# First batch of a Mamba-2 scan with mixer: B and x loaded with two neighbouring tokens to a partition, words reordered

## The chip, the cores and the metric

The kernel runs on one core of one Trainium2 chip. The metric is device time in microseconds (us). Five engines work beside each other, each through its own queue in order: TensorE (PE, with its weight loads PEld), VectorE (DVE), ScalarE (ACT), GpSimd (POOL) and SyncE (SP), whose queue issues nearly all of the DMAs. Engines wait for one another by semaphores.

## What is computed

Two stages follow each other. The first is a scan over 4 batches, 8 heads, 768 tokens, head size 32, state size 16; the second is a mixer over tokens and channels.

```
for each chunk:                       # cum = cumsum(log a) in the chunk
    M = (C B^T) * exp(cum_i - cum_j) * causal
    y = M x  +  (C state) * exp(cum)
    state = exp(sum log a) * state + sum_j exp(cum_last - cum_j) B_j x_j
u = y + (V^T U^T y)                   # along the tokens, rank 32; y as (768, 256)
out = u + relu(u w_ch1) w_ch2
```

The kernel picks its own chunks (64 tokens); the result is the same.

## The kernel before

The scan is cut into twelve *pairs* k = 0 to 11: three pairs of 256 tokens for each of four batches, each with four chunks of 64 tokens. Pairs 0, 1 and 2, the first batch, are called LIGHT and have code of their own; pairs 1, 2 and 3 are SCALED, their products of B and C with the decays are made on POOL (L490), all others on DVE. The steps of a pair:

- loads: `load_bc` (L199) takes B in two DMAs of 64 KB, one for each block of 128 tokens (runs of 64 bytes), and C in one of 128 KB, with tokens 2p and 2p+1 on partition p (runs of 128 bytes). `load_x` (L214) takes x in two DMAs of 128 KB, again a block each (runs of 128 bytes).
- `prep` (words P, Q): BC = B and C times decays F. The decays come from `decays` (L383, words A0 for B and A1 for C, over all four batches) and the chunk factors `kept` from `keep` (word K).
- `turn` (words T, V): transposes on PE, then copies T (ACT) and masked copies Cm (ACT or DVE).
- `gram` (word g): the products of C and B, four PSUM banks of 128x512, one for each pair of heads. For a light pair 16 matmuls with 256 columns.
- `mask` (words M, m): the causal mask. Of the four banks of a light pair DVE takes three with a bitwise and against `lower`, and the fourth goes by an ACT copy (L563) and then POOL: one affine_select over 128x512 (L564) and one memset of a quarter (L567).
- `state` (word s), `update` (word u): the chunk's own state on PE (L598), then on DVE one instruction for each chunk (S), then on POOL the masked states Sm (L626; DVE for later pairs).
- `inter` (words i, j): what the earlier state adds (L672); `intra` (word n): M times x, for light pairs 16 matmuls over all 128 partitions (L694), for the others 32 over 64 partitions (L704). `yout` (word y) copies to yT, `ytokens` (words t, O) transposes back to tokens.

For pairs that aren't light, the two chunks that share a partition row range write different banks, and the second half of `inter` may start only when all earlier products of the pair are done: `apart` (L631) puts a memset of the tile `settled` into POOL's queue, which waits for those products and for which PE waits.

The mixer of a batch (words p, q, a, then U, f, e, h, J, d) uses nearly all of PE's time from then on. Its weights are 64-bit floats which DVE and ACT turn into 32-bit ones piece by piece (word c, steps of `to_fp32`, L424; the pieces of a conversion are taken one by one; loads W, w, Z for V, z for U).

The order of all work is written out by hand, as words: LOADS (L35) is issued first, PLAN (L40) is then followed word by word, and each word puts its instructions at the end of the queues of the engines it uses. So an instruction's place in each queue is the place of its word. F words are matmuls on constants that keep PE busy. All PSUM tiles come from one pool of eight banks. DMAs use eight semaphores in turn, so that an issue on SP waits for the DMA eight before it to have landed.

## Time and profile before

| | us |
|---|---|
| median of three runs (lowest, highest) | 217.02 (216.36, 218.56) |
| the profiled execution: its time, its span | 216.94, 215.1 |
| busy in that span: PE, DVE, ACT, POOL | 207.0, 161.3, 119.9, 14.5 |

A time in a row of the timeline is the start in us from the span's start, then the time that it took; `x3` says that three instructions were merged, and brackets tell the idle time before it and what ended it. A matmul in 32 bits stands as two records. All of DVE's instructions bear the line of a helper, L169, so its rows are told apart by tile.

### The profile page before, as it was taken

What the parts mean: (1) busy time and instruction counts of PE and PEld (TensorE: products, weight loads), DVE (VectorE), ACT (ScalarE), POOL (GpSimd) and SP (SyncE); (2) the same over time, 40 slices, a digit from 0 to 9 for tenths busy, and PEclk for the clock granted to TensorE, in tenths of its full rate; (3) what the DMA queues carried; (4) which work ended last, traced back from release to release, by engine and by line L of the source; (5) the groups of instructions that cost most, each with busy time, mean ns of one, the idle gap of its engine ahead of it and who ended that gap; (6) DMA issues with size and microseconds to landing.
All of it is one profiled execution on the core that took longest, in us unless ns stands there. A gap on an engine that the chain in (4) does not pass through costs nothing.

```text
span 215.1 us, 6853 instructions
## 1 busy us (share of the span) xinstructions
PE 207.0 (96%) x2912; PEld 180.8 (84%) x2912; DVE 161.3 (75%) x334; ACT 119.9 (56%) x273; POOL 14.5 (7%) x46
## 2 busy tenths in 40 slices
PE   7998699999999999999999999999999999999993
PEld 4666465666676989999899999998999999999993
DVE  4679499999999999968977594497347756636942
ACT  3566567896847695655275527433646357357120
POOL 7463210000000000000000000000000000000000
PEclk9999999999999999999999999999999999999999
DMA  5987899998850035002061010100001000100012
GB/s 87 142 184 106 120 202 316 155 265 110 109 80 3 2 66 111 0 3 76 3 81 21 24 49 3 49 27 6 6 0 49 0 27 0 49 29 0 0 50 100
DMA packets 69519, 14.57 MB, mean 68 GB/s; under 512 B 63792, under 2 KB 67696, under 8 KB 69488
## 3 DMA queue, kind: packets, MB, share of 16 engines
q1 hardware_dynamic: 69488, 14.13, 33.6%
q8 instruction: 23, 0.38, 0.8%
q14 instruction: 8, 0.07, 0.1%
HBM read 10.98 MB, written 3.15 MB: 66 GB/s over the span
## 4 chain that ended last, share of the span: by engine, by line
PE 84%; SPq 5%; DMA 4%; DVE 2%; issue 2%; ACT 1%; DVEq 0%
PE x L797 31%; PE z L797 24%; PE y L797 12%; SPq L195 5%; PE y L704 3%; PE y L672 3%; DMA words<-in_moe_w_ch_dram 3%; PE x L547 2%; PE w L728 2%; PE w L506 2%; DMA bc<-in_C_dram 2%; PE w L598 1%; PE w L751 1%; PE z L547 1%; DVE M L169 1%
## 5 line engine op out<-in xcount | busy, mean ns | idle before, releaser
L169 DVE SCALAR_TENSOR_TENSOR words<-words 128x768 fp32r<-128x768 f32 (+6 forms) x48 | 38.0, 818 | 0.7 <-PE y L797 0.5
L797 PE MATMUL z<-u,w 128*128 128x384 f32 x144 | 32.0, 341 | 0.0
L797 PE MATMUL x<-u,w 128*128 128x384 f32 x144 | 31.7, 338 | 0.0
L797 PEld LDWEIGHTS z<-u,w 128*128 128x128 f32 x144 | 24.3, 188 | 0.3 <-issue 0.2
L797 PEld LDWEIGHTS x<-u,w 128*128 128x128 f32 x144 | 24.3, 188 | 0.2
L802 ACT ACTIVATE x<-x 128x384 f32<-128x384 f32 (+1 forms) x32 | 14.3, 448 | 18.1 <-PE x L797 18.1
L802 ACT ACTIVATE z<-z 128x384 f32<-128x384 f32 (+1 forms) x28 | 12.8, 461 | 16.6 <-PE z L797 16.1
L169 DVE SCALAR_TENSOR_TENSOR words<-x,words 128x384 fp32r<-128x384 f32 x24 | 13.1, 553 | 8.7 <-ACT words L831 8.6
L169 DVE SCALAR_TENSOR_TENSOR words<-z,words 128x384 fp32r<-128x384 f32 x24 | 12.9, 552 | 8.9 <-ACT words L831 8.8
L797 PE MATMUL y<-w,words 128*128 128x256 f32 x144 | 19.3, 281 | 0.0
L797 PEld LDWEIGHTS y<-w,words 128*128 128x128 f32 x144 | 18.4, 189 | 0.1
L797 PE MATMUL x<-w,words 128*128 128x256 f32 x128 | 18.3, 281 | 0.0
L797 PE MATMUL x<-w2c,words 128*128 128x256 f32 x96 | 17.6, 317 | 0.0
L797 PEld LDWEIGHTS x<-w,words 128*128 128x128 f32 x128 | 17.0, 188 | 0.2
L797 PEld LDWEIGHTS x<-w2c,words 128*128 128x128 f32 x96 | 14.9, 189 | 1.1
L831 ACT ACTIVATE words<-x 128x384 fp32r<-128x384 f32 x24 | 11.7, 491 | 6.0 <-PE x L797 5.9
L831 ACT ACTIVATE words<-z 128x384 fp32r<-128x384 f32 x24 | 11.6, 492 | 3.0 <-PE z L797 3.0
L169 DVE SCALAR_TENSOR_TENSOR S<-S,kept,w 128x64 f32<-128x64 f32 x40 | 11.1, 278 | 1.6
L797 PE MATMUL z<-yT,w1f 128*128 128x384 f32 x32 | 11.7, 495 | 0.1
L797 PE MATMUL x<-yT,w1f 128*128 128x384 f32 x32 | 11.1, 489 | 0.0
L672 PEld LDWEIGHTS y<-T,Sm 32*64 32x64 f32 x352 | 8.1, 131 | 2.7 <-issue 2.1
L797 PE MATMUL y<-w2c,words 128*128 128x256 f32 x72 | 10.3, 282 | 0.0
(170 smaller groups left out, 398.4 us busy)
## 6 DMA issues: line engine op xcount, KB each, us to landing
words<-in_moe_w_ch_dram SPq DMA_DIRECT2D x7, 512.0 KB, 6.8
x<-in_x_dram SPq DMA_DIRECT2D x24, 128.0 KB, 3.6
out_dram<-ytok SPq DMA_DIRECT2D x24, 128.0 KB, 1.7
bc<-in_B_dram SPq DMA_DIRECT2D x24, 64.0 KB, 3.0
bc<-in_C_dram SPq DMA_DIRECT2D x12, 128.0 KB, 3.1
words<-in_moe_w_ch_dram SPq DMA_DIRECT2D x2, 256.0 KB, 5.5
words<-in_moe_V_dram SPq DMA_DIRECT2D x4, 48.0 KB, 4.8
words<-in_moe_U_dram SPq DMA_DIRECT2D x1, 192.0 KB, 5.0
```

The source lines that it names most:

```text
L169: self.last = call(*args, **kwargs)
L195: op = nc.sync.dma_start(**kwargs)
L506: nc.tensor.transpose(out=tp[:, i, v], in_=s["BC"][:, i, c + v].rearrange("p h n -> p (h n)"), identity=ident)
L547: nc.tensor.matmul(out=g[r][cols, c], lhsT=s["T"][rows, 0, c, cols], rhs=s["Cm"][rows, :, :, ts(2 * c + p, Q)].rearrange("r v t i -> r v i ...
L598: nc.tensor.matmul(out=s["A"][p][ts(r, Q), v], lhsT=s["BC"][half, 0, v, 2 * r:2 * r + 2].rearrange("p h n -> p (h n)"), rhs=x_sb[k][half, ...
L672: product = nc.tensor.matmul(out=y[at][ts(r % 2, H), c, ts(p, H)] if light else y[p][ts(r % 2, H), r // 2, c], lhsT=own[ts(r, Q)], rhs=s[" ...
L704: product = nc.tensor.matmul(out=y[p][ts(i, Q), n, c], lhsT=x_sb[k][half, c, h], rhs=s["M"][half, h // 2, c, h % 2], start=fresh(k, p, [i] ...
L728: nc.tensor.transpose(out=t[:, c, g], in_=yT[b][:, g, ts(2 * q + c, P)], identity=ident)
L751: nc.tensor.matmul(out=p[ts(i % 4, Q), h], lhsT=U_sb[:, c], rhs=ytok[b][:, c, h], start=i < 4, stop=True, skip_group_check=True)
L797: nc.tensor.matmul(out=t, lhsT=lhsT, rhs=rhs, start=start, stop=True, skip_group_check=True)
L802: nc.scalar.activation(t, t, AF.Copy, scale=1.0 + EPS)
L831: nc.scalar.activation(gs[j, m // 2][0][:, m % 2], t, AF.Relu, scale=NEAR)
```

## The change

For the light pairs B and x now lie as C does: partition p holds tokens 2p and 2p+1. B comes in one DMA of 128 KB (runs of 128 bytes), x in one of 256 KB (runs of 256 bytes). LOADS now lists all nine DMAs of the first batch. What follows from the layout:

- `decays`: word A1 makes the factors for C and, by one more ACT instruction, the factors for B of batch 0. A0 is left with batches 1 to 3 and comes later.
- `prep`: for a light pair B in one instruction in place of two.
- masks: `lower` was filled by a memset and two copies on POOL. Now `paired` is made by two affine_selects over 64x256 and two memsets over 32x128 on POOL, and one DVE instruction over 128x256 turns it into `lower`. The fourth bank of a light pair takes two affine_selects over 64x512 and two memsets over 32x256 on POOL in place of one and one.
- `state`: a chunk is 32 partitions with two tokens each: 32 matmuls (32 rows, 32 columns, 64 wide) for a pair in place of 16, in two words s k.0 and s k.1, each with two PSUM banks of its own (four for a pair in place of two).
- `intra`: 32 matmuls over 64 partitions in place of 16 over 128; `inter` follows the new banks, and `apart` now holds for light pairs too: three more memsets on POOL and three more waits of PE.
- all words of PLAN up to about the first U words stand in another order; behind them few words change places.

```diff
 LOADS = (
-    'b0.0 b0.1 b0.2 x0.0 x0.1 b1.0 b1.1 b1.2 ')
+    'b0.0 b0.1 x0.0 b1.0 b1.1 x1.0 b2.0 b2.1 x2.0 ')
 PLAN = (
-    'x1.1 F2.0 A0 b2.1 Q1.0 Q0.0 A1 Q0.1 b2.2 Q1.2 Q0.2 K0 Q1.1 s0 b2.0 V0.0.0 x1.0 V0.1.1 u0.0 '
-    'u0.1 W1 W0 Z0 Q2.2 F2.3 x2.0 F3.3 V1.0.2 b3.2 x2.1 b3.0 Q2.1 b3.1 F3.0 z0 x3.0 x3.1 Q2.0 '
-    'V1.1.2 b4.0 g0 M0 g1 m0 M1 V2.1.2 F2.1 V2.0.2 s1 b4.1 n0 m1 c2 i0 b4.2 j0 u1.0 b5.1 c0 u1.1 '
-    'c0 g2 y0.0 n1 b5.0 M2 i1 s2 w3 y0.1 O0.0 b5.2 m2 j1 u2.0 u2.1 y1.1 w4 P3 y1.0 n2 w5 w2 c0 '
-    'c2 c1 x4.1 i2 c1 c0 j2 T3 y2.0 y2.1 c1 T3 t1 s3 w6 u3.0 x4.0 X5 c1 u3.1 O2.1 g3 M3 o2 m3 v0 '
+    'F2.3 A1 Q1.0 Q0.0 Q0.2 Q1.2 K0 F2.0 s0.0 u0.0 V0.0.0 A0 F3.3 V1.1.2 Q2.0 V0.1.1 V1.0.2 Q2.2 '
+    'F3.0 b3.0 W1 W0 Z0 b3.1 b3.2 s0.1 u0.1 z0 x3.0 x3.1 b5.1 g0 F2.1 M0 m0 w3 g1 M1 m1 V2.1.2 '
+    'V2.0.2 s1.0 u1.0 n0 s1.1 u1.1 g2 c2 i0 j0 b4.0 c2 M2 c0 c0 s2.0 b4.2 n1 s2.1 i1 y0.1 y0.0 '
+    'b5.0 O0.0 c0 m2 n2 b4.1 j1 y1.1 w2 u2.0 y1.0 u2.1 P3 i2 b5.2 c1 c1 c0 j2 y2.1 y2.0 x4.1 T3 '
+    'T3 t1 c1 c1 w4 s3 O2.1 u3.0 u3.1 g3 o2 p0 w5 M3 m3 v0 c2 i3 q0 v1 P4 w6 w8 v2 n3 v3 c2 R0 '
...
@@ load_bc
-            if part == 1:
+            if part == 1 or k in LIGHT:
                 begin(
-                    out=bc_sb[k][:, :, 1].rearrange("p h t n -> p h (t n)"),
-                    in_=C[b, :, ts(q, 2 * P), :].rearrange("h (p t) n -> p h (t n)", t=2))
+                    out=bc_sb[k][:, :, part].rearrange("p h t n -> p h (t n)"),
+                    in_=(B, C)[part][b, :, ts(q, 2 * P), :].rearrange(
+                        "h (p t) n -> p h (t n)", t=2))
@@ load_x
+        if k in LIGHT:
+            x_sb[k] = raw.tile([P, NH, 2, D], FP32, tag="x", name="x")
+            begin(
+                out=x_sb[k].rearrange("p h t d -> p h (t d)"),
+                in_=x[b, :, ts(q, 2 * P), :].rearrange("h (p t) d -> p h (t d)", t=2))
+            return
@@ masks
-    lower = const.tile([P, 2, H], INT32)
-    nc.gpsimd.memset(lower, 0)
+    paired = const.tile([P, 2, P], FP32)
     for v in range(2):
-        half = slice(v * H, v * H + H)
-        nc.gpsimd.tensor_copy(out=lower[half, v], in_=causal[half])
+        nc.gpsimd.affine_select(
+            out=paired[ts(v, H)], in_=ones[ts(v, H), None, :].to_broadcast([H, 2, P]),
+            pattern=[[-1, 2], [1, P]], compare_op=ALU.is_ge, fill=0.0, base=0,
+            channel_multiplier=-2)
+        nc.gpsimd.memset(paired[v * H:v * H + Q, :, H:], 0.0)
+    lower = paired.bitcast(INT32)
+    vector.tensor_scalar(out=lower, in0=paired, scalar1=-1.0, scalar2=None, op0=ALU.mult)
@@ mask, fourth bank
+                    for v in range(2):
+                        nc.gpsimd.affine_select(
+                            out=m[ts(v, H)], in_=m[ts(v, H)], pattern=[[-1, 2], [0, 2], [1, P]],
+                            compare_op=ALU.is_ge, fill=0.0, base=0, channel_multiplier=-2)
+                        nc.gpsimd.memset(m[v * H:v * H + Q, :, :, H:], 0.0)
@@ state
+        if k in LIGHT:
+            own = chunks(k, c, 1)
+            for i in own:
+                A[i] = bank("w", 2 * D)
+            for t in range(2):
+                for r in range(4):
+                    for i in own:
+                        nc.tensor.matmul(
+                            out=A[i][ts(r, Q)],
+                            lhsT=s["BC"][ts(i, Q), 0, t, 2 * r:2 * r + 2].rearrange(
+                                "p h n -> p (h n)"),
+                            rhs=x_sb[k][ts(i, Q), 2 * r:2 * r + 2, t],
+                            start=(t == 0), stop=True, skip_group_check=True)
+            return
@@ inter
-        after = [apart(k)] if part and not light else []
+        after = [apart(k)] if part else []
@@ intra
-                for c in range(2):
+                for t in range(2):
                     for i in range(4):
-                        nc.tensor.matmul(
-                            out=y[n][ts(i, Q), c], lhsT=x_sb[k][:, c, 4 * n + i],
-                            rhs=s["Ms"][n][:, i // 2, c, i % 2], start=fresh(k, n, [i]),
-                            stop=True, skip_group_check=True)
+                        for c in range(2):
+                            product = nc.tensor.matmul(
+                                out=y[c][ts(i, Q), n], lhsT=x_sb[k][ts(c, H), 4 * n + i, t],
+                                rhs=s["Ms"][n][ts(c, H), i // 2, t, i % 2],
+                                start=fresh(k, c, [i]), stop=True, skip_group_check=True)
+                            behind.setdefault(k, []).append(product)
```

## The prediction

> **What bounds the kernel now.** I read the page first, then busy time by stretches, then the chain, then the timelines of the first 33 us, where the change lies.

> ```profile
> span 215.1 us, 6853 instructions
> PE 207.0 (96%) x2912; PEld 180.8 (84%) x2912; DVE 161.3 (75%) x334; ACT 119.9 (56%) x273; POOL 14.5 (7%) x46
> ```

> The table by stretches (columns: PE, PEld, DVE, ACT, POOL busy with counts, clock, DMA share, GB/s) shows three stages.

> ```profile
> 5.00:28.00 23.00, 19.66 (x488) 13.58 (x489) 15.96 (x43) 14.38 (x41) 9.43 (x22) 1.00 0.88 139
> 28.00:80.00 52.00, 51.84 (x871) 37.15 (x869) 50.33 (x114) 39.07 (x84) 1.03 (x5) 1.00 0.66 130
> 80.00:215.00 135.00, 131.87 (x1565) 128.01 (x1557) 92.47 (x164) 64.80 (x149) 0.49 (x5) 1.00 0.13 31
> ```

> From 28 to 80 us DVE (50.33 of 52) and PE (51.84) are both full, and then PE alone (131.87 of 135). Nothing that gets ready earlier there can start earlier. Only before 28 us are all engines partly idle (DVE 7 of 23 us), and there no single engine binds but a chain. So the change is worth what it moves the moment at which the full stage begins. I take two marks for it, the masks M of pair 3 on DVE (28.12) and the first U matmul on PE (32.64, line 797). The chain in order of time:

> ```profile
> 10.52 5.51 DMA words<-in_moe_w_ch_dram
> 16.05 0.98 SPq L195
> ...
> 18.55 3.54 DMA bc<-in_C_dram
> 22.10 2.20 issue
> ...
> 25.95 0.49 ACT T L510
> 26.43 0.75 ACT Cm L516 x2
> ```

> It runs through loads: W1 lands at 16.05, and in that moment SP goes on with its queue; C of pair 3, issued at 18.55, lands at 22.10; POOL then makes BC of pair 3, PE transposes it, ACT copies T and Cm, and `gram` follows at 27.23. The queues themselves:

> ```profile
> 1.25 0.44 SPq L195 DMA_DIRECT2D bc<-in_B_dram  x1
> 10.52 1.09 SPq L195 DMA_DIRECT2D words<-in_moe_w_ch_dram  x2
> 19.18 0.58 SPq L195 DMA_DIRECT2D words<-in_moe_U_dram  x1
> ```
> ```profile
> 5.65 0.94 DVE L169 TENSOR_TENSOR BC<-bc,F 128x128 f32<-128x128 f32 x3 [0.73 <-ACT F L398]
> 12.03 0.69 DVE L169 TENSOR_TENSOR words<-z,lower 128x512 int32<-128x512 int32 x1 [1.79 <-POOL BC L490]
> 14.43 1.28 DVE L169 TENSOR_TENSOR words<-x,lower 128x512 int32<-128x512 int32 x2
> 16.05 0.50 DVE L169 TENSOR_SCALAR words<-words 128x256 int32<-128x256 int32 x2 [0.34 <-DMA words<-in_moe_w_ch_dram]
> 19.90 0.92 DVE L169 SCALAR_TENSOR_TENSOR S<-S,kept,w 128x64 f32<-128x64 f32 x3
> 20.74 1.07 DVE L169 SCALAR_TENSOR_TENSOR words<-words 128x256 f32<-128x256 f32 x2
> 24.41 0.63 DVE L169 TENSOR_SCALAR words<-words 128x384 int32<-128x384 int32 x2 [2.60 <-DMA x<-in_x_dram]
> 28.12 0.76 DVE L169 TENSOR_TENSOR M<-z,causal 128x256 int32<-128x256 int32 x2 [0.30 <-PE z L547]
> ```
> ```profile
> 4.94 0.20 POOL L378 MEMSET lower<- 128x128 int32 x1
> 5.21 0.52 POOL L381 COPY lower<-causal 64x64 int32<-64x64 int32 x2
> 13.35 0.31 POOL L567 MEMSET words<- 64x256 f32 x1
> 20.91 0.62 POOL L626 TENSOR_TENSOR Sm<-S,own 128x192 f32<-128x192 f32 x1 [1.22 <-DVE S L169]
> 22.22 1.10 POOL L490 TENSOR_TENSOR BC<-bc,F 128x512 f32<-128x512 f32 x1 [0.70 <-DMA bc<-in_C_dram]
> ```
> ```profile
> L564 POOL TENSOR_SCALAR_AFFINE_SELECT words<-words x3: 634/635/635, 12.7 to 18.7; 128x512 f32<-128x512 f32 x3
> ```
> ```profile
> 9.57 0.81 PE L148 MATMUL w<-one 128*128 128x384 f32 x2
> 10.53 0.48 PE L537 MATMUL x<-Cm,T 32*64 32x256 f32 x2
> 13.97 0.46 PE L598 MATMUL w<-x,BC 64*32 64x64 f32 x32
> 14.36 1.08 PE L694 MATMUL y<-words,x 128*32 128x128 f32 x32
> 23.37 0.66 PE L506 MATMUL w<-ident,BC 128*128 128x128 f32 x4 [0.90 <-POOL BC L490]
> 27.23 0.35 PE L547 MATMUL x<-Cm,T 32*64 32x128 f32 x2 [0.68 <-ACT Cm L516]
> 27.96 0.86 PE L751 MATMUL x<-ytok,UV 128*32 128x256 f32 x16
> 30.34 0.86 PE L704 MATMUL y<-M,x 64*32 64x64 f32 x64
> 32.64 1.56 PE L797 MATMUL z<-yT,w1f 128*128 128x384 f32 x4
> ```
> ```profile
> 17.36 0.51 ACT L444 ACTIVATE words<-words,bias 128x256 int32<-128x256 int32 x1 [0.17 <-DVE words L169]
> 18.03 0.59 ACT L563 COPY words<-z 128x512 f32<-128x512 f32 x1
> ```

> The reader should see two DMA waits, POOL's 0.70 at 22.22 and DVE's 2.60 before 24.41 (words of U and V: the name x there is the last landing, c1 itself reads U), and beside them a compute chain that is nearly as late: S of pair 2 ends at 20.82, Sm at 21.53, so without any DMA wait BC of pair 3 would have started only 0.7 us earlier. That is the point of this prediction.

> **The change part by part.**

> *Loads.* Before W1, SP issued 13 DMAs (1.31 MB) from 1.25 to 10.52, 0.71 us each, or 139 GB/s. In the new order 10 DMAs (1.64 MB, since x of pair 2 now comes first) stand before W1. If the count of DMAs sets the pace, W1 is issued at 1.25 + 10 x 0.71 = 8.4; if bytes do, at 1.25 + 1.64 MB / 139 GB/s = 13.0. I take 10.7, the middle, and also about what it was. W1 lands 5.5 later: 13.9 to 18.5, taken as 16.2. C of pair 3 now waits for x of pair 2, not for V, and stands before U: it is issued about 12 to 14 and is there before 18, so its wait (22.10) is gone. U now waits for W1's landing directly: landing some 5.1 after that (19.18 to about 24.3 before), 19 to 23.6, taken as 21.3; its words are due on DVE at 22.0.

> *Start.* POOL: in place of the memset and two copies (4.94 to 5.73) two selects of 64x256, between half and the whole of 0.635, taken as 0.40, and two memsets of 128 elements (0.20): with the steps between them until 6.3. DVE makes `lower` from it (0.25, half of the 16.05 row), and this stands in front of BC of pair 0, which started at 5.65. So BC starts at 6.55 and, with the same elements (0.94 less the third start), ends at 7.4 in place of 6.59; its B half, for state 0, at 7.0.

> *PE up to the first gram.* From 7.0: two halves of state 0 (64 records; the 13.97 row gives 0.39 for 32, so 0.78), eight transposes and A0 (about 1.5 by the 23.37 row, 0.66 for four), two F words of 0.7 (0.81 for the two records of the 9.57 row, which overlap what follows): 3.7. Gram of pair 0 starts at 10.75 in place of 10.53. A matmul of state is half as tall and there are twice as many; a record costs 12 ns by the 13.97 row.
> [...]

> *DVE.* First mask 1.50 after the gram: 12.25. Six masks take 3.68 as before (12.03 to 15.71): 15.93. Then pair 1's four S (0.30 each): 17.1; first step of c2 (0.50): 17.6 (W1 is there; at the late end it waits 1.4); mask 0.65, 18.25; first step of c0, 18.75. Now comes a step moved ahead of pair 2's work: c0's third step (1.07, the 20.74 row) needs ACT, which has a copy (0.59), the low words (about 0.5, as much as the power) and the power (0.51) to do after gram 2: 19.2, so it ends at 19.85. Two masks, 21.1; S of pair 2 (0.92), 22.0. It was 20.82: the moved word costs 1.2 us here, and gives it back as work already done.

> *POOL.* The fourth bank takes 2 x (0.635 + 0.31) = 1.9 a pair, not 0.95. From 12.75 the masks of pairs 0 and 1 end at 16.7; n0, at 14.65, needs its own only in its last third; Sm 1, 17.7, settled, pair 2's until 20.3; n2 needs that at 21.1. Hidden. Then Sm 2 (0.62) 22.65, BC 3 (1.10) 23.75, settled (0.10), before j2. The cover is DVE's 22.0: POOL alone would be through at 20.95, 2.8 us earlier.

> *PE behind.* Intra: twice the records, half as tall; the 30.34 row has 64 such records in 0.86 at half the width, so between 0.86 and 2.16 (twice the 14.36 row), taken as 1.08, since the tiles of both halves run beside each other. Each j waits for settled, by estimate 0.4 us (a memset and two semaphores). Behind j0 and j1 stand states and intra that are early anyway; behind j2 stands T3, on the chain. So j2 24.05, T3 24.4, ACT's T and Cm (25.95 and 26.43 rows, 1.3 with start) 26.4, gram 3 26.5, masks M of pair 3 at 27.4 in place of 28.12. From there to U the instructions are the same: 4.52 us, so U at 31.9.

> *Sum.* DMA waits gone (0.7 at POOL, 2.6 at DVE), of which 2.6 are taken up again by the later start (0.2) and S of pair 2 (1.2) and by waits of DVE for gram 3; left over: 32.64 - 31.9 = 0.7. The shift goes through the full stages unchanged. The profiled execution took 216.94 (span 215.1), 0.08 under the median of 217.02: 216.94 - 0.7 = **216.2**.

> **The rivals.**

> *Earlier weights count too (faster).* The big weight loads are asked for earlier (w3 behind the first masks). If DVE's idle time from 28 to 80 (52 - 50.33 = 1.7) came from loads, it goes as well: 216.2 - 1.7 = 214.5. Against it: that idle lies spread over 52 us and mostly behind PE. Chance 0.18.

> *POOL becomes the chain (slower).* The new selects have a pattern of two or three steps on 64 partitions, of which no row here tells the price. With e more for each of 512 elements, POOL's own chain to BC 3 ends at 20.95 + 7.3 e (six selects, and two of 256 at the start). At e = 0.39 it takes over from DVE (23.75); at e = 0.8, a select of 1.43, it is 3 us late, 219.2; at 1.53 it gives 219.9. For it: every settled and Sm stands in the same queue. Against: the three selects of before took 634 to 635 ns, also beside DVE's masks. Chance of over 219.2: 0.20.
> [...]

> *The loads do not get shorter.* W1 at the late end, 18.5: DVE waits 1.4 before pair 2's mask, and all behind it moves: 216.2 + 1.4 = 217.6. With milder forms of the POOL case (217.1 to 219.2) 0.22.

> **How the numbers follow.** The forecast itself, 215.0 to 217.1, has 0.40; its range takes the 0.7 us to lie between nothing and 1.8 (all idle of DVE before M 3 gone). Faster by over 1% (under 214.8; about what a measurement can tell here): 0.18. Slower by over 1% (above 219.2): 0.20. Within: 0.62. Leaving a tenth at each side, the range goes from the faster rival's 214.4 to 219.5.

> **What would show it.** Right: no DMA wait on POOL before BC of pair 3 nor on DVE before the words of U; BC of pair 0 at about 6.5, S of pair 2 ending near 22, M of pair 3 near 27.4, U near 31.9, the stretch behind as long as before. Wrong: selects over 1 us; DVE waiting for W1 at 17; U after 32.6; or a stretch from U to the end that is longer or shorter than before by over 1 us, since then the reordered words behind U count and not the start.

## The result and the profile after

| | before | after |
|---|---|---|
| median, us (lowest to highest) | 217.79 (216.36 to 218.75) | 226.89 (223.66 to 227.72) |
| profiled execution: span | 215.1 | 221.9 |
| first U matmul (the mark U) | 32.64 | 36.87 |
| from there to the end of the span | 182.5 | 185.0 |

The ratio of the times is 1.0335 (95%: 1.0248 to 1.0423). The change made the kernel slower; the forecast was 216.2 us, 0.7 less than before. The profiled execution of after is its fastest, 223.66 us; the other three took 226.53 to 227.72 us, and the ratio leaves two of them out. Of the 6.8 us by which the span grew, 4.2 lie ahead of U and 2.6 behind.

The page of after, first its span, then busy time, the clock by slices, and TensorE's queue of program code (packets, MB, share):

```profile
span 221.9 us, 7227 instructions
PE 211.6 (95%) x3096; PEld 184.7 (83%) x3096; DVE 162.6 (73%) x334; ACT 119.8 (54%) x274; POOL 18.0 (8%) x54
...
PEclk9999699999999999999999999999999999999999
...
q8 instruction: 24, 0.39, 0.7%
```

There are 184 more records of matmul and as many of weight load (92 matmuls), and a dip of the clock in a slice (22 to 28 us) where before has none. Up to 18 us the timelines go as foretold within 0.7 us (DVE, then POOL, then PE); the steps of c0 on VectorE (19.06 and 20.11) then take longer:

```profile
6.46 0.76 DVE L169 TENSOR_TENSOR BC<-bc,F 128x256 f32<-128x256 f32 x2
...
12.54 0.69 DVE L169 TENSOR_TENSOR words<-z,paired 128x512 int32<-128x512 int32 x1 [0.60 <-PE z L552]
...
17.70 0.49 DVE L169 TENSOR_SCALAR words<-words 128x256 int32<-128x256 int32 x2
...
19.06 0.94 DVE L169 TENSOR_SCALAR words<-words 128x256 int32<-128x256 int32 x2
20.11 1.20 DVE L169 SCALAR_TENSOR_TENSOR words<-words 128x256 f32<-128x256 f32 x2
...
22.43 1.03 DVE L169 SCALAR_TENSOR_TENSOR S<-S,kept,w 128x64 f32<-128x64 f32 x3
23.83 0.63 DVE L169 TENSOR_SCALAR words<-words 128x384 int32<-128x384 int32 x2 [0.37 <-DMA bc<-in_B_dram]
...
29.08 1.06 DVE L169 SCALAR_TENSOR_TENSOR words<-words 128x384 f32<-128x384 f32 x2 [4.29 <-ACT words L457]
...
32.26 0.76 DVE L169 TENSOR_TENSOR M<-z,causal 128x256 int32<-128x256 int32 x2 [0.36 <-PE z L562]
```
```profile
4.86 0.40 POOL L386 TENSOR_SCALAR_AFFINE_SELECT paired<-ones 64x256 f32<-64x256 f32 x1
...
13.24 0.63 POOL L580 TENSOR_SCALAR_AFFINE_SELECT words<-words 64x512 f32<-64x512 f32 x1 [0.54 <-ACT words L578]
...
19.15 0.68 POOL L580 TENSOR_SCALAR_AFFINE_SELECT words<-words 64x512 f32<-64x512 f32 x1 [0.31 <-ACT words L578]
...
24.76 0.10 POOL L662 MEMSET settled<- 128x1 f32 x1 [3.37 <-PE y L701]
24.95 0.51 POOL L655 TENSOR_TENSOR Sm<-S,own 128x192 f32<-128x192 f32 x1
25.42 1.10 POOL L505 TENSOR_TENSOR BC<-bc,F 128x512 f32<-128x512 f32 x1
```
```profile
20.05 1.16 PE L724 MATMUL y<-words,x 64*32 64x128 f32 x64
21.14 0.42 PE L614 MATMUL w<-x,BC 32*32 32x64 f32 x16
21.49 0.35 PE L701 MATMUL y<-T,Sm 32*64 32x64 f32 x6
23.95 0.69 PE L701 MATMUL y<-T,Sm 32*64 32x64 f32 x10 [2.11 <-issue]
24.57 1.11 PE L758 MATMUL x<-ident,yT 128*128 128x128 f32 x4
25.62 1.88 PE L724 MATMUL y<-words,x 64*32 64x128 f32 x64
```

The last fence shows where most of it is lost. In the middle of one product of pair 1, between its sixth record and its seventh, TensorE stands still for 2.11 us and waits for nothing that another engine does ("issue"). Then 64 records of intra, which took 1.16 us in the pair before, take 1.88. The other engines hang on it: POOL's settled waits 3.37 for this product, ScalarE's copies wait behind it, and VectorE waits 4.29 for a step of the conversion that stands behind those copies. The table by stretches gives the clock (the third figure from the end: 1.00, 0.97, 0.50, 0.68):

```profile
20.00:22.00 2.00, 1.85 (x104) 1.35 (x86) 1.89 (x4) 0.42 (x2) 1.27 (x3) 1.00 0.97 186
22.00:24.00 2.00, 0.05 (x4) 0.05 (x4) 1.42 (x5) 0.00 (x0) 0.00 (x0) 0.97 1.03 197
24.00:26.00 2.00, 2.00 (x30) 1.55 (x38) 0.79 (x3) 0.28 (x1) 1.16 (x3) 0.50 0.49 57
26.00:28.00 2.00, 2.00 (x96) 1.70 (x80) 0.00 (x0) 0.35 (x2) 0.52 (x1) 0.68 0.78 106
```

Most of the 2.6 us behind U are in one place too, where TensorE's order is the same in both kernels. Before, then after:

```profile
100.13 0.51 PE L598 MATMUL w<-x,BC 64*32 64x64 f32 x32
100.58 0.78 PE L672 MATMUL y<-T,Sm 32*64 32x64 f32 x32
```
```profile
104.34 0.51 PE L627 MATMUL w<-x,BC 64*32 64x64 f32 x32
104.78 0.34 PE L701 MATMUL y<-T,Sm 32*64 32x64 f32 x3
107.35 0.77 PE L701 MATMUL y<-T,Sm 32*64 32x64 f32 x29 [2.23 <-issue]
```

**Theory A.** TensorE runs out of program. Its queue q8 moved 24 packets and 0.39 MB, so 16 KB each. A 32-bit matmul is 4 instructions (two records each of matmul and load), and TensorE's queue has 6249 records in all (57 of them semaphores and drains), some 260 to a packet. Counted in order, 961 records are done at the first stop and 3777 at the second, 2816 apart, which is 11 times 256; A takes a packet for a block of 256 instructions. The packet belonging to the first stop was under way as it began (packet 21.19 to 22.60, stop 21.84 to 23.95): in the stretches 19.4 to 21.1, 21.1 to 22.7 and 22.7 to 23.9 the queue table names q8 in the second only:

```profile
q1 hardware_dynamic: 238, 0.33, 92.4%
q8 instruction: 1, 0.02, 5.5%
```

By A a block is asked for only when a border ahead of it has been passed, and TensorE stops where it is through with the instructions that it has before the next block is there. The packets fit that. Put a border at every 256th record, counted from the stops (193, 449, 705, 961 and so on), and take packets and borders in order: each of the 24 packets of after starts 1.03 to 6.61 us behind the record that stands 64 ahead of its border (before: 23 packets, 1.25 to 5.49 us). Against the border's own record seven start early in each kernel, by up to 2.61 us, so the asking runs ahead of TensorE's records. How far is an estimate from these starts: they scatter least with some 64 records in after and 48 in before. From the record 256 ahead of a stop to the stop's end it took 4.6 and 3.9 us in after. So by A it counts how many instructions stand close together and where the borders fall.

**Rivals.** B: the new order, POOL's queue and the new waits make the start late, and the stop is only a sign. C: the weight load w3, asked for at 19.3, crowds out the fetch. D: the dummies with which A is tested cost time by themselves.

### The profile page after: what moved, and what is told of

Same layout as the page of the kernel before. It is cut to its first block, busy times and chain, and to the rows that moved or that the text cites. A ratio compares the mean times of both kernels' runs of the same rounds, so it can differ in the third digit from the quotient of the medians.

```text
span 221.9 us, 7227 instructions
## 1 busy us (share of the span) xinstructions
PE 211.6 (95%) x3096; PEld 184.7 (83%) x3096; DVE 162.6 (73%) x334; ACT 119.8 (54%) x274; POOL 18.0 (8%) x54
## 3 DMA queue, kind: packets, MB, share of 16 engines
q1 hardware_dynamic: 63248, 14.13, 32.3%
## 4 chain that ended last, share of the span: by engine, by line
PE 86%; DVE 5%; issue 3%; DMA 2%; ACT 1%; SPq 0%; POOL 0%; DVEq 0%
PE x L827 27%; PE z L827 23%; PE y L827 12%; PE y L701 4%; PE y L735 2%; PE x L562 2%; PE w L521 2%; PE y L724 2%; PE w L758 2%; DVE words L169 2%; DMA x<-in_x_dram 1%; PE x L552 1%; PE w L781 1%; PE w L614 1%; DMA a_sb<-in_a_dram 1%
## 5 line engine op out<-in xcount | busy, mean ns | idle before, releaser
L169 DVE SCALAR_TENSOR_TENSOR words<-words 128x768 fp32r<-128x768 f32 (+6 forms) x48 | 38.2, 822 | 5.0 <-ACT words L457 4.3
L827 PE MATMUL z<-u,w 128*128 128x384 f32 x144 | 32.2, 341 | 0.0
L827 PE MATMUL x<-u,w 128*128 128x384 f32 x144 | 31.5, 338 | 0.0
L827 PEld LDWEIGHTS x<-u,w 128*128 128x128 f32 x144 | 24.3, 188 | 0.2
L832 ACT ACTIVATE x<-x 128x384 f32<-128x384 f32 (+1 forms) x32 | 14.4, 449 | 16.7 <-PE x L827 16.7
L832 ACT ACTIVATE z<-z 128x384 f32<-128x384 f32 (+1 forms) x28 | 12.8, 461 | 16.2 <-PE z L827 15.7
L169 DVE SCALAR_TENSOR_TENSOR words<-z,words 128x384 fp32r<-128x384 f32 x24 | 12.9, 551 | 10.2 <-ACT words L861 10.1
L169 DVE SCALAR_TENSOR_TENSOR words<-x,words 128x384 fp32r<-128x384 f32 x24 | 13.1, 553 | 8.4 <-ACT words L861 8.2
L827 PE MATMUL x<-w2c,words 128*128 128x256 f32 x96 | 17.6, 317 | 0.0
L701 PE MATMUL y<-T,Sm 32*64 32x64 f32 x352 | 12.4, 238 | 5.0 <-issue 4.3
L701 PEld LDWEIGHTS y<-T,Sm 32*64 32x64 f32 x352 | 9.6, 133 | 8.4 <-issue 6.4
L169 DVE SCALAR_TENSOR_TENSOR S<-S,kept,w 128x64 f32<-128x64 f32 x40 | 11.1, 278 | 2.6 <-PE w L614 0.7
L662 POOL MEMSET settled<- 128x1 f32 x12 | 1.2, 101 | 128.7 <-PE y L701 70.8
```

The costliest lines, as they stand in the source:

```text
L169: self.last = call(*args, **kwargs)
L701: product = nc.tensor.matmul(out=y[inner][ts(r % 2, H), r // 2, ts(p, H) if light else c], lhsT=own[ts(r, Q)], rhs=s["T"][ts(r, Q), 1, :, ...
L827: nc.tensor.matmul(out=t, lhsT=lhsT, rhs=rhs, start=start, stop=True, skip_group_check=True)
L832: nc.scalar.activation(t, t, AF.Copy, scale=1.0 + EPS)
```

## The experiments

**Moving the borders.** A function puts dummy matmuls (4 instructions each) early in the stream, into a PSUM bank that is not in use yet:

```diff
-    warm(3, "x")
+    def pad(n, w):
+        t = bank("x", 4 * P)
+        idle(t, w)
+        for i in range(n):
+            c = i % 4
+            nc.tensor.matmul(out=t[ts(c, Q), :1], lhsT=one[:Q].to_broadcast([Q, Q]),
+                             rhs=one[:Q], start=True, stop=True, skip_group_check=True)
+
+    pad(54, 1)
```

After with n = 54:

> The kernel after, with 54 matmuls of 32x32 by one column on a PSUM bank that nobody reads yet, early in TensorE's stream, in place of two of three warming matmuls; results and order of the words are unchanged, but everything behind stands 216 TensorE instructions later in the program. Theory A (the two stops of TensorE, 2.1 us inside the inter product of pair 1 and 2.2 us at 105 us, are the fetch of its program in blocks of 16 KB, or 256 instructions, so that where a stop falls depends on where a block ends in the stream): both stops are gone, the clock does not fall to half behind the first, M of pair 3 comes at 28.5 to 29.5 in place of 32.26, U at 32.5 to 34, time 217 to 220. Theory B (the new order of the words causes the late start, TensorE's stop is only its sign): M of pair 3 stays at 31.5 to 32.5, U at 36 to 37, time 223 or more.

Measured: 223.31 us, ratio to before 1.0298 (1.0247 to 1.0349). The stops moved but did not go: 0.47 at 20.8, 1.32 at 25.4, 0.95 at 34.9 and 1.91 at 106.9. The forecast of A for this kernel failed. It had been reckoned on the timeline of after with its own stops in it, so that the blocks looked slower to consume than they are. The reckoning was then fitted anew to these stops, and a fit shows nothing by itself; the later runs test it. What the trace does show is the count: 961, 1217, 1729 and 4033 records are done at the four stops, all of them whole blocks of 256 from the two counts of after.

Before with n = 28:

> The kernel before, with 28 such matmuls (112 TensorE instructions) in place of one of three warming matmuls. Theory A: the block borders move to places that were harmless in the kernel after: a stop of about 2 us appears in a dense run of inter products near 101 us, perhaps one of 1.4 us near 143 us, the first 33 us stay as they were (U at 32.6); time 219 to 221. Theory B, or any theory in which the stops belong to the new order or the new layout: no stop, 217 to 218.

Measured: 221.19 us, 1.0187 (1.0121 to 1.0254). As A said: the kernel before gets a stop without anything of the change, and in the same product as after, split at the same record:

```profile
101.78 0.34 PE L680 MATMUL y<-T,Sm 32*64 32x64 f32 x3
103.88 0.77 PE L680 MATMUL y<-T,Sm 32*64 32x64 f32 x29 [1.76 <-issue]
```

(92 added matmuls are 368 instructions; less 256 that is 112, as many as 28 dummies.) A smaller stop that was not foretold, 0.60 at 25.1, and the dummies' own time made U 0.95 later. After the late stop the clock was at half from 104.8 to 108.3 us.

The control, after with n = 8:

> Control for the first: the kernel after with only 8 such matmuls (32 TensorE instructions), all warming matmuls kept. Theory A: the borders fall 32 instructions earlier in each run, so both stops stay, each eight records nearer to the start of its run, 1 to 2.2 us long; time 222 to 227. A theory in which any dummy work at the start, or another rhythm of the first microseconds, is what helps: time falls as with 54, to 217 to 220.

Measured: 224.33 us, 1.0313 (1.0243 to 1.0384), inside A's range and not the rival's. Of the two stops foretold at 1 to 2.2 us the late one is there (2.19 at 104.9). The early one failed: in the light pairs there are two short ones (0.73 at 19.3, 0.16 at 22.9), and U came at 34.79. One more that was not foretold (0.98 at 157.5) and the clock at half from 106.3 to 109.7 us let the stretch behind U grow to 187.5.

Before with n = 64, a whole block:

> The kernel before with 64 of the dummy matmuls, 256 TensorE instructions, which is just one block of 16 KB. Theory A (what counts is where the block borders fall): the borders fall where they fell in the kernel before, so no stop, 216.5 to 218, though there are more than twice the dummies of the run with 28, which had stops of 0.60 and 1.76 us. Rival D (the dummies themselves, the time that they take, or the longer program, are what costs): at least as slow as with 28 of them, 221 to 224.

Measured: 217.84 us, 1.0018 (0.9974 to 1.0061); no stop at all. With more than twice the dummies of the run with 28 the time is that of before, so D falls; the dummies do make U 0.64 later (33.28).

After with n = 36:

> The kernel after with 36 dummies, 144 instructions. Theory A, now with a block's price from the runs so far (from the border, as the queue 64 instructions ahead sees it, to the next block being there: 4.4 us in the first 40 us, when loads fill the rings, 3.85 behind): the stop near 105 us is gone; in the light pairs a stop of about 1.5 us stays near 23 us, since there more than 256 instructions stand in less time wherever the border falls; U at 34.5 to 36.5; time 219 to 221.5. Rival D: as with 8 or 54 dummies, 223 to 224.5.

Measured: 223.19 us, 1.03 (1.0246 to 1.0354). That a block costs more early fits the 4.6 and 3.9 us of after; that the loads make it so is the author's estimate (DMA share 0.97 and 1.03 from 20 to 24 us there). Half right. The stop near 105 us is gone, and from U to the end it takes 182.5 us, as in before. But the light pairs got worse than the reckoning said, stops of 0.55, 1.03 and 2.12 us, with the clock at half until 34 us, and U at 39.34:

```profile
27.16 1.07 PE L732 MATMUL y<-words,x 64*32 64x128 f32 x22 [2.12 <-issue]
```
```profile
28.00:31.00 3.00, 2.69 (x58) 2.22 (x53) 0.98 (x2) 2.10 (x6) 0.10 (x1) 0.50 1.01 228
31.00:34.00 3.00, 3.00 (x50) 2.17 (x56) 1.53 (x6) 1.93 (x6) 0.00 (x0) 0.50 0.39 93
```

**Taking the instructions out, and putting them in.** First after with the matmuls of before in number:

```diff
 state
-            for t in range(2):
+            for t in range(1):
...
+            for i in own:
+                nc.tensor.matmul(out=A[i][:Q], lhsT=ident[ts(i, Q), ts((i + 1) % 4, Q)],
+                                 rhs=ident[ts(i, Q), :2 * D], start=False, stop=True, skip_group_check=True)
 intra
-                for t in range(2):
+                for t in range(1):
...
+            product = nc.tensor.matmul(
+                out=y[0][:Q], lhsT=ident[:H, ts(2, Q)],
+                rhs=ident[:H, None, :].to_broadcast([H, 2, P]),
+                start=False, stop=True, skip_group_check=True)
+            behind.setdefault(k, []).append(product)
```

> The kernel after, leaving out part of the computation: in state and intra of the light pairs only the first of the two tokens of a partition is multiplied, 16 matmuls a word pair in place of 32 as before the change; TensorE's time is put back by few wide matmuls on zeros (four of 64 columns for the states, one of 256 for intra, for each pair), and 50 dummies early bring the whole stream to 256 instructions over that of the kernel before. Loads, masks, POOL's work, settled and the order of the words stay those of after. Theory A (the number of TensorE instructions in the light pairs is what costs): no stop over 0.5 us, M of pair 3 at 28 to 29.5, U at 32.3 to 33.8, time 216.5 to 218.5. Theory B (order, POOL, new waits): U at 34 or later, time 219 or more.

Measured: 218.86 us, 1.0124 (1.0052 to 1.0197). Masks, POOL, settled, loads and order are those of after, and the loss is nearly gone: one stop of 0.28 us at 82, no dip of the clock, 182.9 us behind U. M of pair 3 is at 29.68 and U at 34.29, 0.2 and 0.5 us beyond A's range (the time by 0.4), and U is 1.65 later than in before, of which the dummies are 0.64 by the run with 64. So B holds about 1.0 us, and no more.

Then the reverse, before with 92 more matmuls that compute nothing:

```diff
 state
+                if k in LIGHT:
+                    nc.tensor.matmul(
+                        out=s["A"][p][ts(r, Q), v, :1], lhsT=zero[half, :Q], rhs=zero[half, :1],
+                        start=False, stop=True, skip_group_check=True)
...
 intra
+                        nc.tensor.matmul(
+                            out=y[n][ts(i, Q), c, :1], lhsT=zero[:, :Q], rhs=zero[:, :1],
+                            start=False, stop=True, skip_group_check=True)
```

> The kernel before, with one matmul on zeros, 32 columns by 1, added behind each matmul of state and intra of the light pairs, 92 in all, as many as the change adds; results, loads, masks and order are those of before. Theory A: stops appear in the light pairs, 1 to 2.5 us together, and one of about 2 us near 103 us, since the borders behind stand as in after; U at 33.5 to 36, time 220 to 224. Theory B: the order of the words and POOL are those of before, so U at 32.6 to 33.3 and 217 to 218.5.

Measured: 223.82 us, 1.0331 (1.026 to 1.0401): as large a loss as the whole change's (1.0335), from as many added matmuls, with old loads, layout and order. The span is 222.2 (after: 221.9) and U 36.24, 0.24 beyond A's range. Of the loss some 0.9 us may be the added matmuls' own time, an estimate from the 0.64 that 64 dummies cost. A short stop, 0.44, is at 158.3, and the two long ones stand where those of after stand, with 961 and 3777 records done:

```profile
23.79 0.26 PE L600 MATMUL w<-x,BC 64*32 64x64 f32 x3 [1.60 <-issue]
...
106.41 0.78 PE L678 MATMUL y<-T,Sm 32*64 32x64 f32 x30 [1.90 <-issue]
```

**The order.** After with 54 dummies, and c0's third step moved back:

```diff
-    ... b5.0 O0.0 c0 m2 n2 b4.1 j1 y1.1 w2 u2.0 y1.0 u2.1 P3 i2 ...
+    ... b5.0 O0.0 m2 n2 b4.1 j1 y1.1 w2 u2.0 y1.0 u2.1 c0 P3 i2 ...
```

> The first kernel (54 matmuls), with the third step of c0 on VectorE moved back from ahead of the second mask word of pair 2 to behind its state update, ahead of P3. If that step's 1.07 us is a term of what is left of the later start: S of pair 2 ends 0.8 to 1.1 us earlier, M of pair 3 and U 0.5 to 1.1 us earlier than in the first kernel, time 0.5 to 1.1 us less. If POOL's queue or the loads hold the start, S of pair 2 moves and U does not: time as the first kernel's, within 0.3. Theory A also says for this one: no stop, as the stream of TensorE is unchanged.

Measured: 224.06 us, 1.0317 (1.0265 to 1.0369). S of pair 2 came 1.17 earlier (22.01 in place of 23.18), U 1.09 earlier (35.44), and the time did not fall: a stop of 1.86 at 105.7 was followed by the clock at half this time (from 105.9 to 109.3 us), which one of 1.91 in the kernel without the move was not. A's "no stop" failed here as it did there; there are six. The same move in the kernel with few matmuls:

> The kernel that multiplies only the first token of each partition in the light pairs' state and intra (so part of the computation is left out, as before), now with c0's third step behind pair 2's state update and not ahead of its masks. It tells what holds U at 34.29 there. If it is the moved step (1.2 us on VectorE, as the prediction had it): S of pair 2 starts at 22.1 to 22.5 in place of 23.33, M of pair 3 and U come 0.7 to 1.3 us earlier, time 0.7 to 1.3 us less. If it is POOL's longer queue (its masks and Sm) or the words of U: S of pair 2 moves, U stays within 0.4 us.

Measured: 218.29 us, 1.0063 (1.0034 to 1.0092). S of pair 2 at 22.12, U at 33.47, 0.82 earlier, the span 0.6 shorter, with one stop of 0.30 at 150.9. What then stands between it and before, 0.83 at U, is about what the dummies cost (0.64).

**The loads.** After with w3 later:

```diff
-    ... g0 F2.1 M0 m0 w3 g1 ... y1.1 w2 u2.0 ...
+    ... g0 F2.1 M0 m0 g1 ... y1.1 w3 w2 u2.0 ...
```

> The kernel after with the load w3 (512 KB) asked for behind y1.1, ahead of w2, and not at 19.3 us behind the first masks; TensorE's stream is the same. Rival C (the fetch of TensorE's program is late at 21 to 24 us because the weight load fills the DMA rings): the fetch takes under 1.1 us in place of 1.41, the first stop is at most 1.2 us in place of 2.1, U 1 to 2 us earlier, 221 to 222. Theory A without C (a block costs about as much anyway): the first stop is 1.7 to 2.2 us, U within 0.5 us of 36.87, time as after's, 223 to 225; the stop at 105 us stays in both.

Measured: 226.67 us, 1.0354 (1.029 to 1.042), no faster than after. The fetch took 1.19 in place of 1.41 and the first stop 1.56 in place of 2.11, both between the two ranges. A new stop of 1.29 came at 30.3, and the one near 105 us stayed (2.19). U came at 38.87, two stretches at half clock ahead of it, so neither forecast of U held. C can have some tenths in it; it doesn't carry the loss.

Before with V asked for later:

```diff
-    ... W1 W0 Z0 Q2.2 F2.3 x2.0 ... b3.1 F3.0 z0 x3.0 ...
+    ... W1 W0 Q2.2 F2.3 x2.0 ... b3.1 F3.0 z0 Z0 x3.0 ...
```

> The kernel before with one thing changed: the four small loads of V are asked for behind the loads of pair 3 and U and not ahead of pair 2's second half, so that C of pair 3 and U are asked for some 2.5 us earlier, which is what the change did with its loads, without its layout and order; TensorE's stream is the same. If the two waits for loads before 25 us are worth what the prediction said: the wait of POOL for C of pair 3 (0.70) and most of VectorE's 2.60 go, U at 31.9 to 32.2, 216.3 to 216.9, or 0.4 to 0.8 less than before. If nothing hangs on them, or W1 lands as much later as C lands earlier: U at 32.5 or later, time as before or more.

Measured: 218.37 us, 1.0063 (1.0034 to 1.0093), 0.6% slower than before. The edit did less than was meant: C of pair 3 was asked for at 17.23 (18.55 before) and U at 18.53 (19.18). POOL did start BC of pair 3 without a wait, 0.58 earlier, but U came only 0.17 earlier (32.47): TensorE now waited for x of pair 3, asked for later, and VectorE still 1.95, now for V. So it is no clean test of what the two waits are worth. Behind U the stretch took 184.2 us, 1.7 more without a stop; what costs that was not followed up.

```profile
21.64 1.28 POOL L491 TENSOR_TENSOR BC<-bc,F 128x512 f32<-128x512 f32 x1
```
```profile
25.91 0.35 PE L599 MATMUL w<-x,BC 64*32 64x64 f32 x16 [0.79 <-DMA x<-in_x_dram]
```

**The counts.** The traces leave no other cause for the stops. In ten of the thirteen kernels there are 29 stops of 0.16 us and more with "issue" in front, and in every one the number of TensorE's records done before it, divided by 256, leaves the same remainder, 193. TensorE goes on 1.2 to 1.6 us after a packet of q8 has come in, in all 29 (1.35 and 1.36 in after). The other three kernels, before itself and before with 64 dummies or with V later, have no such stop.

## Why the prediction was wrong

The step that failed is *PE behind*, with its last sentence in the sum, "The shift goes through the full stages unchanged". It priced 92 more matmuls by the time of their records alone, 12 ns each for the states and 17 for intra (1.08 for 64), and asked only whether an engine was late. That the instructions have to be brought in was not in the sum, and no rival had it. The runs showed stops of 2.11 and 2.23 us there, and 1.17 us for work at half clock behind the first.

- *Loads*: right. W1 was asked for at 9.6 (10.7 foretold), nobody waited for it, and POOL did not wait for C of pair 3. U was asked for at 15.20 and landed 4.3 later, at 19.5 (21.3), so the 0.37 of VectorE before its words is no wait for it; the same 0.36 to 0.38 stand there in five other kernels.
- *Start*: right. BC at 6.46 (6.55), gram at 11.08 (10.75).
- *DVE*: right in kind, too small in size. S of pair 2 ended at 23.46, where 22.0 was foretold. The moved step costs 1.17 to 1.21 us there, as the prediction had it (1.2), and 0.82 to 1.09 at U. Part of the rest is a slip (a step of 1.07 from 19.2 on ends at 20.27, not 19.85) and part was left out: c0's first step took 0.94, and 0.49 in before (at 17.04), while a select of POOL (0.68 from 19.15) ran beside it, and the third 1.20 beside the next select. That the selects slow VectorE fits these rows; no run tests it by itself.
- *POOL*: right that it is not the chain. The selects took 0.40 and 0.63 to 0.72, so e is near nothing, and the kernel with POOL's whole work but few matmuls has U 1.65 later than before, 0.64 of it for the dummies, and not 4.2.
- *Intra and states*: the records took what was foretold (1.16 for 64 of intra, 1.08 foretold; 0.45 for 32 of states), until the stop. The 0.4 for a wait on settled had no row for its semaphores; the trace of after has two such waits of TensorE, 0.5 together, the longest 0.3.
- *The gain of 0.7*: not there. With the count taken out U is at 34.29, or 33.65 without the dummies' 0.64: 1.0 later than in before, mostly c0's step, not 0.7 earlier. So U would have missed its 31.9 without the stops too, by less.
- *From U on*: wrong by 2.57 us, one stop of 2.23 in it. The bound named for this, over 1 us, was passed.

The 6.8 us, as the runs divide them: 2.11 first stop and 1.17 for work at half clock behind it (1.11 for 0.66, 1.88 for 1.16 in two rows), together 3.3 of the 4.2 ahead of U; the remaining 1.0 the order, mostly c0's step (the kernel with the count taken out divides it the same way: its 33.65 lies 3.2 ahead of 36.87); 2.6 behind U, where before is free of the stop only by where its borders fall: with 28 dummies it has it too. That the instruction count and the borders cause the stops is shown from both sides (the two kernels with the count exchanged, and the two of before with 28 and with 64 dummies) and by the counts. How long a stop gets at a given place is not settled: for 36 dummies the reckoning gave 1.5 us in the light pairs, and 3.7 were measured. No alignment of after was found that is free of stops in the light pairs, and no version that beats before.

## What to carry to other kernels

Count instructions, not only engine time: in after TensorE was through with 256 of them (64 small 32-bit matmuls) in 2.5 and 1.7 us and with the stops behind them it took 4.6 and 3.9, so the fetch of its program was a bound of its own, and 92 more matmuls, split or on zeros, brought that about. It need not be one: in before the 256 records from 77.66 to 79.98 us (2.3 us) end at a border, behind a slower stretch (13.4 us for the 256 ahead of them), and there is no stop. Wherever "issue" stands in front of a group that is cut in the middle, compare the instruction counts of such places before looking for a wait. And a difference of one per cent or two between two kernels with different instruction counts may be where the borders fall (before with 28 dummies took 1.0187 of its time, with 64 of them 1.0018); a few dummies, and then a whole block of them, tell it apart.
